# Issuing the attention part's weight loads from ScalarE's queue instead of SyncE's

## The chip, the cores and the metric

The kernel runs on one core of a Trainium2 chip. The time is device time of one execution in microseconds (us). Names used below: PE is TensorE (matrix products), DVE is VectorE, ACT is ScalarE, POOL is GpSimd and SP is SyncE, which here only issues DMAs.

## The reference

Three computations follow each other; the second and third take the output of the one before as `x`.

```python
# attention: q, k, v are (2, 8, 768, 64); blocks of 32 keys, window of 16
k_sum = k.reshape(B, H, nb, block, D).max(axis=3)
v_sum = v.reshape(B, H, nb, block, D).mean(axis=3)
scores_l = scale * np.matmul(q, k.transpose(0, 1, 3, 2))      # kept where |i - j| < window
scores_s = scale * np.einsum('bhsd,bhnd->bhsn', q, k_sum) + np.log(block)
a = softmax over [scores_l (masked), scores_s]
x = np.matmul(a, np.concatenate([v, v_sum], axis=2))          # -> (1536, 512)
# first feed-forward part: w_in 512 x 2048, w_out 2048 x 512
h = x @ w_in
x = (h - np.tanh(h)) @ w_out
# second: w1, w2 512 x 1024, w3 1024 x 1024, w_out 1024 x 512
out = ((x @ w1) * (x @ w2)) @ w3 @ w_out
```

Inputs and outputs are float32.

## The kernel before

All weights come to the chip as 64-bit words and are turned into float32 by the engines. A **unit** is one 128 x 512 block of a weight; there are 72, in a fixed order (first `w3` and the last `w_out`, whose product is formed during attention, then `w_in`, `w_out`, `w1`, `w2`). A unit goes through these steps, all in class `Weights`:

- `load`: a DMA of 512 KB into one of four buffers `raw` (`NRAW = 4`).
- `start`: ACT forms `bits` (in some units `dec`) from the words' upper halves (L112).
- `dve`: three DVE instructions (L115, L117, L119) make the float32 block `dec`. The third is the last that reads `raw`.
- `high`: ACT rounds it to `wh` (L147). `low`: POOL forms the rest `wl` (L154).

Attention runs in 28 steps `g` (0 to 27), a loop written out by hand; the order in which the code names instructions is each engine's order. A step works on several groups of four tiles at once: scores of group g + 1 (PE, `s`), softmax of group g (DVE `pr`, `nm` at L374, then four exponentials on ACT at L377), transposes of g - 2 (PE, `t`, L391) and their copy to SBUF at the end of the step (ACT, `pt`, L396), values of g - 3 (PE, `av`, L406), the split of the result of g - 4 (ACT `xh` at L417, DVE `xl`). There is one PSUM tile for `t`, so the transposes of a step wait until ACT has copied those of the step before. Three steps make one pair of heads. Beside this a step decodes one unit; steps 15, 18, 21, 24 and 25 start two (`MORE`). Pieces of the weight product (`w34a`) fill PE.

SP issues all DMAs, in the order of the code: keys `kt`, queries `qt`, values `vg`, the block means' rows (`vg` from `vr`, three small DMAs a pair), and the weights' `raw`. `load` lets a unit's DMA go when fewer than four buffers are taken:

```python
while len(self.raws) < min(n, len(self.units), self.n_dve + NRAW):
```

`n_dve` counts units whose three DVE instructions have been issued; `dve` calls `load` right behind the third. So the DMA that refills a buffer stands in SP's queue as soon as the code has named that third instruction, and SP waits there until DVE has executed it.

Of the kernel before, what the change touches and what calls it, by code (L numbers as in the profile page):

```python
# [46 lines left out]
NRAW = 4  # L47
# [10 lines left out]
def fused_kernel(tc, qT, kT, vW, w_in, w_out, w1, w2, w3, wo2, out):  # L58
    nc = tc.nc
    mm = nc.tensor.matmul  # L60

    class Weights:


        def __init__(self):
            self.units, self.index, self.raws, self.t, self.parts = [], {}, [], [], []
            self.free, self.place, self.ahead, self.psum, self.one = [], [], 1, None, False
            self.ops = []
            self.n_dve = self.n_high = self.n_low = 0

        def add(self, key, src):
# [17 lines left out]
            return place, *(pool.tile([P, 512], dt, tag=t, bufs=bufs, name=f"{name}_{i}") for i, t in enumerate((th, tl)))  # L89

        def load(self, n):
            while len(self.raws) < min(n, len(self.units), self.n_dve + NRAW):
                raw = rawp.tile([P, 512], U64, tag="raw", name=f"raw_{len(self.raws)}")
                nc.sync.dma_start(out=raw, in_=self.units[len(self.raws)])
                words = raw[:, :].bitcast(U32).rearrange("p (n two) -> p n two", two=2)
                self.raws.append((words[:, :, 0], words[:, :, 1]))

# [26 lines left out]
        def dve(self, k=1):  # L124

            for _ in range(k):
                if self.n_dve == len(self.t):
                    return False
                self.ops[self.n_dve].pop(0)()
                if not self.ops[self.n_dve]:  # L130
                    self.n_dve += 1
                    self.load(len(self.t) - 1 + self.ahead)
            return True

        def unit(self, k=1):
# [32 lines left out]
    wt = Weights()  # L168
# [30 lines left out]
    with tc.tile_pool(name="base", bufs=1) as base, \  # L199
# [79 lines left out]
        with tc.tile_pool(name="p1", bufs=1) as p1, \  # L279
# [4 lines left out]
            def load_k(n):  # L284
                kt[n] = p1.tile([P, SG], F32, tag="kt", bufs=3, name=f"kt_{n}")
                w = NQ // 2 * CW
                for i in ((0, w), (w, SG)) if n == 0 else ((0, SG),):
                    nc.sync.dma_start(out=kt[n][:, i[0]:i[1]], in_=kT[n // NP, n % NP, :, i[0]:i[1]])

            def load_q(n):  # L290
                qt[n] = p1.tile([P, S], F32, tag="qt", bufs=2, name=f"qt_{n}")
                w = TU * QT
                for i in ((0, w), (w, S)) if n == 0 else ((0, S),):
                    nc.sync.dma_start(out=qt[n][:, i[0]:i[1]], in_=qT[n // NP, n % NP, :, i[0]:i[1]])

            def load_vwin(n):
                vg[n] = p1.tile([P, NQ, P], F32, tag="vg", bufs=3, name=f"vg_{n}")
                nc.sync.dma_start(out=vg[n], in_=vW[n // NP, n % NP])
# [38 lines left out]
            def block_rows(n):  # L337
                w = NB // NBR
                for c in range(NBR):
                    nc.sync.dma_start(out=vg[n][QT + c * w:QT + (c + 1) * w, :, :],  # L340
                                      in_=vrow[n][c * BLK:c * BLK + w, :].unsqueeze(1).to_broadcast([w, NQ, P]))
# [8 lines left out]
            def scores(g):  # L350

                nonlocal n_s
                n, u = divmod(g, NU)
                st[g] = []
                for _ in range(1 + (g >= ALL)):
                    tag = "extra" if g >= ALL and n_s % 3 == 2 else "s"
                    n_s += g >= ALL
                    st[g].append(ps1.tile([P, TU, NC], F32, tag=tag, bufs=2 if tag == "s" else 1, name=f"s_{g}_{n_s}"))
                wt.one = g >= ALL
                for i in range(TU):  # L360
                    t = u * TU + i
                    for hf in range(2):
                        r = slice(hf * QT, (hf + 1) * QT)
                        mm(out=st[g][i % len(st[g])][half_of(g, i, hf), i, :], lhsT=qt[n][r, t * QT:(t + 1) * QT],
                           rhs=kt[n][r, t * CW:t * CW + NC], start=True, stop=True)
# [76 lines left out]
            for g in range(NG + 4):  # L442
                n, u = divmod(g, NU)
                parts = list(range(n34, min(n34 + N34[g], 32)))
                n34 += len(parts)

                if u == (0 if n else 2) and n + 2 < NN:
                    load_k(n + 2)
                if u == 1 and n + 1 < NN:
                    load_vwin(n + 1)  # L450
                if u == 2 and 0 < n < NN:
                    block_rows(n)
                if u == 2 and n + 2 < NN:
                    load_q(n + 2)

                late = g + 1 >= ALL
                if g + 1 < NG and not late:
                    scores(g + 1)
                for i in parts[:0 if late else 1]:
                    w34_part(i)  # L460
                if 0 <= g - 2 < NG:
                    transposes(g - 2)
                for i in parts[0 if late else 1:]:
                    w34_part(i)
                if g + 1 < NG and late:
                    scores(g + 1)
                if 0 <= g - 4 < NG:
                    x_high(g - 4)
                for i in list(pvs):
                    value_copy(i)  # L470
                if g == 1:
                    value_blocks(0, ps1.tile([P, TU * QT + P], F32, tag="av", bufs=1, name="pvs")[:, TU * QT:])
                if g == 2:
                    block_rows(0)
                if 0 <= g - 3 < NG:
                    rest = values(g - 3)
                    if u == 0 and n < NN:
                        value_blocks(n, rest)
                if g < 2:
                    busy(4)  # L480

                wt.high()
                wt.low()
                for i in range(TU):
                    if g < NG:
                        softmax_a(g, (0, 2, 1, 3)[i] if g >= ALL else i)
                    if i == 1 and 1 <= g <= NG:
                        softmax_b(g - 1)
                    if i == 2 and 0 <= g - 4 < NG:
                        x_low(g - 4)  # L490
                    if i and g < NG + 3:
                        wt.dve(1)
                if g - 1 in MORE:
                    wt.unit()
                if g == NG:
                    wt.psum = None
                if g < NG + 3:
                    wt.start(2 if g in MORE else 1)
                if n + 1 < NN:
                    for i in ((0, 1), (2,), ())[u] if n else ((), (0, 1, 2), ())[u]:  # L500
                        key_blocks(n + 1, i)
                if 0 <= g - 2 < NG:
                    probs(g - 2)
                wt.ahead = min(NRAW, g + 2)
                for i in parts:
                    w34_end(i)
# [405 lines left out]
```

## Time and profile before

| | |
|---|---|
| runs | 582.7, 582.71, 581.56 us, median 582.7 |
| profiled execution, span | 583.9 us |
| PE busy in the span | 567.7 us, 97% |
| DVE, ACT, POOL busy | 463.0, 339.4, 281.2 us |
| DMA | 56.56 MB, mean 97 GB/s |

The profile shows one execution; its span is the time from its first to its last instruction, and nothing of it lies outside. It is 1.2 us longer than the median of the runs. A busy share is a mean over stages that differ much, so the stages have to be read apart.

### The profile page before, as it was taken

Reading aid. Unit: us, or ns where it says so; the run is one execution under the profiler, and the core shown is the slowest. Engines: PE = TensorE matmul, PEld = TensorE weight load, DVE = VectorE, ACT = ScalarE, POOL = GpSimd, SP = SyncE. Lnnn points to the kernel's source line nnn. Section 1 sums busy time; section 2 is a strip of 40 time slices with the busy share of each in tenths; the row PEclk is TensorE's granted clock in tenths of the full one; section 3 lists DMA queues with packets and bytes.
Section 4 is the critical chain, followed back from the end, with each engine's and each line's share of the span. In section 5 each row is a group of like instructions: output and inputs, shape, how many; then the busy total and the mean of one; then the engine's idle time right before and its main releaser. Section 6 shows DMA issues by size and latency. Waiting matters only on the chain.

```text
span 583.9 us, 9222 instructions
## 1 busy us (share of the span) xinstructions
PE 567.7 (97%) x3240; PEld 459.6 (79%) x3240; DVE 463.0 (79%) x885; ACT 339.4 (58%) x741; POOL 281.2 (48%) x239
## 2 busy tenths in 40 slices
PE   7999899999999999999999999999999999999997
PEld 5777677777688888888888888888887887888885
DVE  4699998876999999779999978999658587778610
ACT  3599988856788786466767566764324322213110
POOL 4366555552555655324646522547725644616320
PEclk9999999999999999999999999999999999999999
DMA  8889977540333223012223101233000100000021
GB/s 317 278 299 290 305 243 212 150 158 22 107 107 108 82 100 109 0 36 74 88 93 90 56 1 39 86 92 109 0 1 1 60 13 1 1 1 0 1 90 54
DMA packets 18526, 56.56 MB, mean 97 GB/s; under 512 B 1968, under 2 KB 4656, under 8 KB 18480
## 3 DMA queue, kind: packets, MB, share of 16 engines
q1 hardware_dynamic: 18480, 55.98, 29.4%
q8 instruction: 25, 0.41, 0.3%
q14 instruction: 21, 0.17, 0.1%
HBM read 51.64 MB, written 3.15 MB: 94 GB/s over the span
## 4 chain that ended last, share of the span: by engine, by line
PE 73%; DVE 13%; issue 6%; ACT 4%; DMA 2%; POOL 1%; SPq 0%; DVEq 0%; POOLq 0%; ACTq 0%
PE x L191 6%; PE x L192 6%; PE x L190 6%; PE ph L190 6%; PE ph L192 6%; PE ph L191 6%; PE p_w L190 4%; PE p_w L192 4%; PE p_w L191 4%; PE o L190 3%; PE o L192 3%; PE o L191 3%; PE w L192 2%; PE w L191 2%; PE w L190 2%
## 5 line engine op out<-in xcount | busy, mean ns | idle before, releaser
L154 POOL TENSOR_TENSOR wl<-dec,wh 128x512 fp32r<-128x512 f32 x72 | 110.8, 1543 | 55.1 <-ACT wh L147 51.2
L195 POOL TENSOR_TENSOR gl<-g,gh 128x512 fp32r<-128x512 f32 x48 | 65.2, 1359 | 133.4 <-ACT gh L550 70.9
L191 PE MATMUL x<-gl,wh 128*128 128x512 f32 x192 | 75.1, 391 | 1.7 <-POOL gl L195 1.7
L190 PE MATMUL x<-gh,wh 128*128 128x512 f32 x192 | 75.0, 390 | 0.1
L190 PE MATMUL ph<-xh,wh 128*128 128x512 f32 x192 | 74.8, 390 | 0.0
L192 PE MATMUL x<-gh,wl 128*128 128x512 f32 x192 | 74.7, 389 | 0.0
L192 PE MATMUL ph<-xh,wl 128*128 128x512 f32 x192 | 74.7, 389 | 0.0
L191 PE MATMUL ph<-xl,wh 128*128 128x512 f32 x192 | 74.7, 389 | 0.0
L119 DVE SCALAR_TENSOR_TENSOR dec<-raw,dec 128x512 uint32<-128x512 uint32 x48 | 62.8, 1309 | 1.6
L563 ACT ACTIVATE u<-ph 128x512 f32<-128x512 f32 x48 | 28.8, 599 | 47.9 <-PE ph L192 47.9
L147 ACT CAST wh<-dec 128x512 fp32r<-128x512 f32 x72 | 44.6, 623 | 17.8 <-DVE dec L119 17.6
L571 DVE TENSOR_TENSOR g<-ph,u 128x512 f32<-128x512 f32 x48 | 32.7, 682 | 21.0 <-ACT th L564 20.9
L377 ACT ACTIVATE pr<-pr,nm 128x120 f32<-128x120 f32 x96 | 37.1, 391 | 12.2 <-DVE nm L374 11.9
L191 PEld LDWEIGHTS x<-gl,wh 128*128 128x128 f32 x192 | 36.0, 188 | 10.2 <-POOL gl L195 2.7
L195 POOL TENSOR_TENSOR s_w<-s_w,s_w 128x512 fp32r<-128x512 f32 x16 | 22.9, 1450 | 43.5 <-ACT s_w L742 23.5
L555 DVE COPY_PREDICATED g<-mk,th 128x512 f32<-128x512 uint32 x48 | 39.7, 827 | 4.2 <-DVE g L573 0.5
L190 PEld LDWEIGHTS x<-gh,wh 128*128 128x128 f32 x192 | 36.0, 188 | 8.5 <-DVE x2a L599 0.5
L190 PEld LDWEIGHTS ph<-xh,wh 128*128 128x128 f32 x192 | 36.0, 188 | 7.6
L191 PEld LDWEIGHTS ph<-xl,wh 128*128 128x128 f32 x192 | 36.0, 188 | 7.5
L192 PEld LDWEIGHTS ph<-xh,wl 128*128 128x128 f32 x192 | 36.0, 188 | 7.4
L192 PEld LDWEIGHTS x<-gh,wl 128*128 128x128 f32 x192 | 36.0, 188 | 7.3
L573 DVE SCALAR_TENSOR_TENSOR g<-sq,g 128x512 f32<-128x512 f32 x48 | 39.3, 820 | 0.7 <-ACT sq L569 0.6
(157 smaller groups left out, 1422.2 us busy)
## 6 DMA issues: line engine op xcount, KB each, us to landing
raw<-w SPq DMA_DIRECT2D x32, 512.0 KB
raw<-w_in SPq DMA_DIRECT2D x16, 512.0 KB
raw<-w_out SPq DMA_DIRECT2D x16, 512.0 KB
vg<-vW SPq DMA_DIRECT2D x8, 768.0 KB
raw<-wo SPq DMA_DIRECT2D x8, 512.0 KB
kt<-kT SPq DMA_DIRECT2D x7, 544.0 KB
qt<-qT SPq DMA_DIRECT2D x7, 384.0 KB
out<-u_out SPq DMA_DIRECT2D x6, 256.0 KB
```

The costliest lines, as they stand in the source:

```text
L119: lambda tu=tu, su=su, lo=lo: stt(out=tu, in0=lo, scalar=29, in1=su, op0=ALU.logical_shift_right, op1=ALU.bitwise_or)])
L147: nc.scalar.copy(out=h, in_=self.t[n])
L154: nc.gpsimd.tensor_tensor(out=l, in0=self.t[self.n_low], in1=h[:, :].bitcast(F32), op=ALU.subtract)
L190: mm(out=acc, lhsT=lh, rhs=rh, start=start, stop=False)
L191: mm(out=acc, lhsT=lh, rhs=rl, start=False, stop=False)
L192: mm(out=acc, lhsT=ll, rhs=rh, start=False, stop=stop)
L195: eng.tensor_tensor(out=out, in0=x, in1=high.bitcast(F32), op=ALU.subtract)
L377: nc.scalar.activation(out=pr[g][:, i, :], in_=pr[g][:, i, :], func=AF.Exp, scale=-1.0, bias=nm[g][:, i:i + 1], accum_out=z[g][:, i:i + 1])
L555: nc.vector.copy_predicated(out=g, mask=mask[:, :].bitcast(U32), data=t)
L563: nc.scalar.activation(out=u, in_=ph, func=AF.Square)
L571: nc.vector.tensor_tensor(out=gn, in0=ph, in1=u, op=ALU.mult)
L573: nc.vector.scalar_tensor_tensor(out=gn, in0=sq, scalar=GAM, in1=gn, op0=ALU.add, op1=ALU.mult)
```

## The change

The DMAs of the units from the third on, as long as attention lasts (up to step 23), are issued by ACT. `load` is no longer called when DVE's third instruction has been named, but once a step, behind `low`, and by `start`. In the attention part the limit is no longer `n_dve` but `safe`, the value that `n_dve` had behind `low` of the step. Keys, queries, values and block rows stay on SP, and so do the first two units and all from step 24 on.

```diff
-            self.ops = []
+            self.ops, self.safe = [], 0
...
         def load(self, n):
-            while len(self.raws) < min(n, len(self.units), self.n_dve + NRAW):
+            early = self.psum is not None
+            while len(self.raws) < min(n, len(self.units), (self.safe if early else self.n_dve) + NRAW):
                 raw = rawp.tile([P, 512], U64, tag="raw", name=f"raw_{len(self.raws)}")
-                nc.sync.dma_start(out=raw, in_=self.units[len(self.raws)])
+                (nc.scalar if early and len(self.raws) > 1 else nc.sync).dma_start(out=raw, in_=self.units[len(self.raws)])
...
                 if not self.ops[self.n_dve]:
                     self.n_dve += 1
-                    self.load(len(self.t) - 1 + self.ahead)
+                    if self.psum is None:
+                        self.load(len(self.t) - 1 + self.ahead)
...
                 wt.high()
                 wt.low()
+                wt.load(len(wt.t) - 1 + wt.ahead)
+                wt.safe = wt.n_dve
```

What it does to the order, at three places. Lines of the changed kernel are numbered one to four higher than those of the kernel before. The numbers behind the names count tiles, so the same unit may have another number before and after. In brackets stand the semaphores that a row waits for: `DVE`, `PE`, `Activation`, `Pool` are counted by an engine, `DMAHW` and a digit by earlier DMAs.

ACT in step 6 before: a rounding, the four exponentials, `bits` of the unit loaded three steps ago, the copy `pt`.

```order
L147 CAST wh_568<-dec_457 128x512 [waits DVE_49]
L377 ACTIVATE pr_573,z_574<-pr_573,nm_572 128x120 [waits DVE_49] x4
L112 ACTIVATE bits_593<-raw_387 128x512 [waits DMAHW4_49]
L396 COPY pt_598<-t_541 120x512 [waits PE_49,Activation_49]
L417 CAST xh_124<-av_547 128x256 [waits PE_49]
```

ACT in step 6 with the change:

```order
L149 CAST wh_566<-dec_455 128x512 [waits DVE_49]
L379 ACTIVATE pr_571,z_572<-pr_571,nm_570 128x120 [waits DVE_49] x4
L95 DMA raw_588<-wo 128x512 [waits DMAHW5_49,Activation_49]
L113 ACTIVATE bits_591<-raw_453 128x512 [waits DMAHW6_49]
L398 COPY pt_596<-t_539 120x512 [waits PE_49,Activation_49]
L419 CAST xh_124<-av_545 128x256 [waits PE_49]
```

One DMA stands between the last exponential and `bits`. There are 27 such DMAs on ACT in all: one or two in steps 1 to 23.

ACT in steps 23 and 24 before. `raw_1757` and `raw_1762` are the two units that step 24 starts; SP issued them in steps 21 and 22.

```order
L377 ACTIVATE pr_1812,z_1813<-pr_1812,nm_1811 128x120 [waits DVE_49] x4
L112 ACTIVATE bits_1832<-raw_1687 128x512 [waits DMAHW1_49,DVE_49]
L396 COPY pt_1834<-t_1774 120x512 [waits PE_49,Activation_49]
L417 CAST xh_126<-av_1794 128x256 [waits PE_49]
L147 CAST wh_1863<-dec_1764 128x512
L112 ACTIVATE dec_1876<-raw_1757 128x512 [waits DMAHW2_49,Pool_49]
L112 ACTIVATE dec_1878<-raw_1762 128x512 [waits DMAHW3_49,Pool_49]
L396 COPY pt_1880<-t_1836 120x512 [waits PE_49]
```

ACT in steps 23 and 24 with the change:

```order
L379 ACTIVATE pr_1808,z_1809<-pr_1808,nm_1807 128x120 [waits DVE_49] x4
L95 DMA raw_1825<-w_out 128x512 [waits DMAHW5_49,Activation_49]
L95 DMA raw_1827<-w_in 128x512 [waits Activation_49]
L113 ACTIVATE bits_1830<-raw_1758 128x512 [waits DMAHW2_49,DVE_49]
L398 COPY pt_1832<-t_1770 120x512 [waits PE_49,Activation_49]
L419 CAST xh_126<-av_1790 128x256 [waits PE_49]
L149 CAST wh_1861<-dec_1760 128x512
L113 ACTIVATE dec_1876<-raw_1825 128x512 [waits DMAHW5_49,Pool_49]
L113 ACTIVATE dec_1878<-raw_1827 128x512 [waits DMAHW6_49,Pool_49]
L398 COPY pt_1880<-t_1834 120x512 [waits PE_49]
```

The two units of step 24 are issued in step 23, as a pair. Steps 17 and 20 issue a pair in the same way, for steps 18 and 21.

SP around steps 14 to 17 before: each group of keys, values or block rows stands behind a weight load that waits for DVE.

```order
L340 DMA vg_801<-vr_1025 8x12x128 [waits DMAHW4_49]
L294 DMA qt_1072<-qT 128x768 [waits DMAHW5_49,PE_49]
L94 DMA raw_1127<-w 128x512 [waits DMAHW6_49,DVE_49,Activation_49]
L288 DMA kt_1136<-kT 128x1088 [waits DMAHW7_49,Pool_49]
L94 DMA raw_1211<-w 128x512 [waits DMAHW0_49,DVE_49,Activation_49]
L298 DMA vg_1223<-vW 128x1536 [waits DMAHW1_49,PE_49]
L94 DMA raw_1286<-w 128x512 [waits DMAHW2_49,DVE_49,Activation_49]
L94 DMA raw_1291<-w 128x512 [waits DMAHW3_49,DVE_49,Activation_49]
L340 DMA vg_1002<-vr_1253 8x12x128 [waits DMAHW4_49,PE_49,Activation_49]
```

SP at the same place with the change:

```order
L342 DMA vg_799<-vr_1023 8x12x128 [waits DMAHW3_49]
L296 DMA qt_1070<-qT 128x768 [waits DMAHW5_49,PE_49]
L290 DMA kt_1134<-kT 128x1088 [waits DMAHW6_49,Pool_49]
L300 DMA vg_1221<-vW 128x1536 [waits DMAHW7_49,DMAHW1_49,PE_49]
L342 DMA vg_1000<-vr_1251 8x12x128 [waits DMAHW1_49,PE_49,Activation_49]
```

The weight loads with their waits for DVE are gone from SP here; the rest keeps its order.

## Rows read from the trace of the kernel before

**Rows 1.** Stretch, us, busy PE, PEld, DVE, ACT, POOL (count), PE clock, DMA share, GB/s.

```profile
23.50:74.00 50.50, 46.32 (x594) 36.65 (x595) 47.47 (x199) 46.77 (x161) 30.20 (x30) 1.00 0.92 304
74.00:131.00 57.00, 54.60 (x579) 42.73 (x579) 48.28 (x147) 43.63 (x129) 31.88 (x28) 1.00 0.62 187
131.00:583.90 452.90, 447.34 (x1956) 365.97 (x1954) 357.71 (x499) 240.30 (x423) 210.27 (x143) 1.00 0.16 53
```

**Rows 2.** Waits of ACT, 23.5 to 74: us in total, times, longest.

```profile
ACT pr L377 <- DVE nm L374: 2.5, 8, 0.5
```

**Rows 3.** Waits of all engines, 5 to 131: us in total, times, longest.

```profile
PE t L391 <- ACT pt L396: 3.3, 5, 0.9
...
PE av L406 <- DMA vg<-vr: 1.0, 1, 1.0
...
ACT bits L112 <- DMA raw<-w: 0.6, 1, 0.6
```

**Rows 4.** Waits of SP's DMA queue, 23.5 to 131.

```profile
SPq L94 <- DVE dec L119: 85.3, 28, 15.0
```

**Rows 5.** Line 94: DMA issues, ns min/median/max, first and last start.

```profile
L94 SPq DMA_DIRECT2D raw<-w x32: 327/328/1634, 4.6 to 404.6; - x32
```

**Rows 6.** Timeline of SP's issues at four places: start us, us, instruction.

```profile
34.49 0.33 SPq L94 DMA_DIRECT2D raw<-wo  x1
34.92 0.38 SPq L288 DMA_DIRECT2D kt<-kT  x1
...
109.48 0.33 SPq L94 DMA_DIRECT2D raw<-w_out  x1
111.93 0.33 SPq L94 DMA_DIRECT2D raw<-w_in  x1
...
150.74 0.33 SPq L94 DMA_DIRECT2D raw<-w_out  x1
```

**Rows 7.** Timeline of ACT in step 6; in brackets idle time ahead and its cause.

```profile
37.69 0.40 ACT L377 ACTIVATE pr<-pr,nm 128x120 f32<-128x120 f32 x1 [0.18 <-DVE nm L374]
...
38.08 0.64 ACT L112 ACTIVATE bits<-raw 128x512 f32<-128x512 f32 x1
```

**Rows 8.** Line 396 from 36.5 to 39 us: ns, start; ACTq is ACT's sequencer.

```profile
L396 ACTq EVENT_SEMAPHORE  x1: 17/17/17, 37.7 to 37.7; - x1
L396 ACT COPY pt<-t x1: 575/575/575, 38.7 to 38.7; 120x512 f32<-120x512 f32 x1
```

**Rows 9.** Timeline of ACT and PE around the end of step 17.

```profile
84.12 0.40 ACT L377 ACTIVATE pr<-pr,nm 128x120 f32<-128x120 f32 x1 [0.65 <-DVE nm L374]
...
84.71 0.66 ACT L112 ACTIVATE bits<-raw 128x512 f32<-128x512 f32 x1
...
86.03 0.62 PE L391 MATMUL t<-ident,pr 128*120 128x128 f32 x4 [0.73 <-ACT pt L396]
```

**Rows 10.** Line 112 from 83 to 85 us.

```profile
L112 ACTq EVENT_SEMAPHORE  x1: 17/17/17, 84.1 to 84.1; - x1
```

**Rows 11.** Half microseconds behind the lone load at 150.74, columns as in rows 1.

```profile
151.00:151.50 0.50, 0.50 (x4) 0.42 (x3) 0.50 (x2) 0.50 (x2) 0.10 (x1) 1.00 0.00 0
...
153.50:154.00 0.50, 0.42 (x1) 0.11 (x1) 0.50 (x2) 0.50 (x2) 0.49 (x1) 1.00 0.09 33
```

**Rows 12.** Timeline of ACT and PE, steps 23 to 25.

```profile
114.51 0.40 ACT L377 ACTIVATE pr<-pr,nm 128x120 f32<-128x120 f32 x1 [0.42 <-DVE nm L374]
...
116.94 1.24 ACT L112 ACTIVATE dec<-raw 128x512 f32<-128x512 f32 x2
118.09 0.56 ACT L396 COPY pt<-t 120x512 f32<-120x512 f32 x1
...
120.32 0.65 PE L391 MATMUL t<-ident,pr 128*120 128x128 f32 x4
```

**Rows 13.** The stretch with the highest DMA rate, columns as in rows 1.

```profile
10.00:15.00 5.00, 4.83 (x26) 3.42 (x24) 4.31 (x17) 3.80 (x16) 0.99 (x1) 1.00 1.02 420
```

**Rows 14.** Groups of DVE's instructions, 23.5 to 74: busy us, mean ns, idle ahead.

```profile
L117 DVE SCALAR_TENSOR_TENSOR bits<-raw,bits 128x512 uint32<-128x512 uint32 x13 | 8.9, 686 | 0.0
```

## The prediction, made before the changed kernel ran

> **What bounds the kernel now.** I read the stretches first [rows 1]. Behind 131 us TensorE (PE) is busy 447.34 of 452.90 us, nothing moves to ScalarE there, and only a later start of that part could change it. From 74 to 131 us PE is busy 54.60 of 57.00. From 23.5 to 74 us no engine is full: PE 46.32, VectorE (DVE) 47.47 and ScalarE (ACT) 46.77 of 50.50, and DMA has its highest share, 0.92. There DVE sets the pace and ACT follows closely: ACT's idle time is mostly the wait of the step's fourth exponential for its maximum, 2.5 us in 8 waits [rows 2].
>
> Then the waits from 5 us to 131 us [rows 3]. The reader is to see how few name a DMA: PE once for the rows of block means, 1.0 us, and ACT once for a weight load, 0.6 us. Keys and queries are in neither row. SyncE's queue does spend 85.3 us waiting for DVE's last decode step before it may refill a weight buffer [rows 4], and keys, queries and values stand behind these waits; but nothing behind them was late except the one row of 1.0 us. What PE does wait for is ACT's copy of the transposed probabilities: 3.3 us in 5 waits. Three of these lie in steps 17, 20 and 23.
>
> **What the change removes.** SyncE's queue loses 27 of its loads and their waits, so keys, values and block rows are issued earlier. Worth at most the 1.0 us of PE above. PE and ACT then had slack: that wait lies in the stretch that DVE paces. I take 0. The Trainium skill says in "DMA: Bandwidth & Descriptors", section "Issuing engines are not separate DMA queues", that DMAs of several engines run on the same 16 DMA engines and that issuing from more of them saves only the sequencer's issue time. By that rule the gain is 0 too, and the waits in the trace agree: SyncE's time was not what anyone waited for.
>
> **What it adds on ACT.** 27 issues. ACT issued no DMA before, so the price is bounded by SyncE's: a weight load's issue takes 328 ns in the median, 1634 ns at most [rows 5], and two in a row start 0.43 us apart [rows 6]. I take 0.33 and 0.43, since no wait for space in a queue is likely with one or two loads of 512 KB in ACT's own.
>
> Do they lie beside ACT's work? In step 6 the fourth exponential starts at 37.69, its accumulator is read, and `bits` starts at 38.08 [rows 7]. So 0.39 us pass in which the engine works and its sequencer is free. That the sequencer does run ahead can be seen from an instruction that only the sequencer executes: the semaphore wait ahead of the copy `pt` stands at 37.7, while the copy runs at 38.7 [rows 8]. It was held up to the exponential's release (37.69), then passed it, the accumulator read and `bits` at once. In step 17 the same: the exponential is released at 84.12, and the wait ahead of `bits` stands at 84.1 [rows 9, 10]. So an issue that stands between the exponential and `bits` begins about at the exponential's release and ends 0.33 us later, under the 0.39 us that the engine needs. One issue costs 0 in all steps with one. If this cover were gone, each would push `bits`, `pt`, `xh` and `wh` back by 0.43 us; behind them wait DVE's `xl`, GpSimd's low part and PE's transposes.
>
> Steps 17, 20 and 23 issue two. Both end at 0.05 + 0.43 + 0.33 = 0.81 us behind the release. In step 17 `bits` starts now 0.59 us behind it (84.71), so it moves by 0.22 us, `pt` too, and PE's transposes, which start at 86.03 after waiting 0.73 us for `pt` [rows 9], start that much later. PE goes on from there without slack. 3 x 0.22 = 0.66 us.
>
> The issues carry waits of their own: for a DMA some eight places earlier in the program, which by the steps landed long before, and for ACT's own reading of the buffer. They no longer wait for DVE, since a load is issued only when DVE was done a step before. I take 0.
>
> **What it moves: loads come later.** A buffer is refilled a step later than before, two steps ahead of its use where one unit is started a step. A step lasts 50.5 / 13 = 3.9 us in the first stretch [rows 14]. What a lone load takes: issued at 150.74, its bytes flow from 151.5 to about 153.6 [rows 6, 11], 2.9 us. In time, also with keys and values beside it. But where steps start two units, the lead is one step. The tight one is step 24: its two loads were issued at 109.48 and 111.93 [rows 6]; now both leave ACT in step 23, behind the exponential released at 114.51, that is at 114.55 and 115.0. They are wanted at 116.94 and, 0.57 us on, 117.51 [rows 12]. The first lands at 114.55 + 2.9 = 117.45 at the earliest. The second follows in the same queue, with a third load on SyncE's queue beside it: at best 512 KB more at 420 GB/s [rows 13], 1.25 us, so 118.7; if all three (1.57 MB, 3.75 us at that rate, flowing from 115.4) share, 119.2, and 0.4 us for its slow beginning gives 119.6. So `pt`, at 118.09 now, starts between 119.3 and 120.2 and ends 0.56 us later, at 119.9 to 120.8. PE's transposes of step 25 start at 120.32 now; with step 23's 0.22 they would at 120.54. More delay: 0 to 0.35 us, I take 0.15.
>
> **The sum.** 0 - 0 + 0.66 + 0.15 = +0.8 us. The profiled execution has 583.9 us; it becomes 584.7. It lies 1.2 us above the median of the runs, 582.7, so for runs 583.5 us.
>
> **The rivals.** *ACT pays each issue in full (slower).* If `bits` can't be prepared during an issue and the engine stands still, the double issues cost 84.12 + 0.39 + 2 x 0.43 - 84.71 = 0.66 us each [rows 9], 2.0 us together. The 13 single ones in the first stretch (13 decodes, so 13 steps [rows 14]) cost 13 x 0.43 = 5.6 us, less ACT's idle time there, 50.50 - 46.77 = 3.7 [rows 1]: 1.9. Busy records overlap a little (the exponential's ends at 37.69 + 0.40 = 38.09, `bits` starts at 38.08, with the reading of the accumulator between them [rows 7]), so there is more idle time than that; I take 1.0. With 0.4 of step 24: +3.4 us, 586.1. It decides from an issue time of about 0.45 us on. Against it stand rows 8 and 10; for it, that no DMA was ever seen on this engine.
>
> *The sequencer isn't even held by the exponential.* Then both issues of a pair are over before it is released and steps 17, 20 and 23 lose nothing; step 24's loads leave some 0.5 us earlier, and nothing is left: 582.7. The Trainium skill draws it so in "Perfetto Trace Analysis", section "Per-instruction lifecycle: what the profiler-reported window actually captures": ScalarE instructions are pushed into a wait queue, and the sequencer decodes on while they wait. The trace disagrees in part: 84.1 in rows 10 is the release, not earlier.
>
> *Loads are late at more places.* Values are now issued when PE frees their buffer, in step 17 beside two weight loads. 768 KB more in front of the second one is 1.8 us at 420 GB/s; if PE had no slack there, and step 24 took its worst, +1.5 to +2 us, 584.5.
>
> *Unblocked keys and values pay (faster).* The 1.0 us of PE's wait goes, and ACT's wait behind it: -1.0 us, 581.7; to be faster beyond what can be told it would need a second such place, and no row shows one.
>
> **How the numbers follow.** Within 0.2% (1.2 us, about what a measurement of this kernel tells from no change) are 581.5 to 583.9. Chances: the forecast 0.42, of which 0.08 ends above; the sequencer fully ahead 0.13; ACT pays in full 0.28, all above; late loads 0.07, above by a half; faster 0.10, of which 0.07 by more than 0.2%. Sums: faster 0.07, same 0.53, slower 0.40. The forecast's own range is 582.7 to 584.3. The 8 in 10 must reach to the rival at 586.1 and nearly to the one at 581.7, so 581.8 to 586.2.
>
> **What would show it.** On ACT: DMA issues of 0.33 us in the profile that lie beside the exponential, `bits` 0.39 us behind the fourth exponential's start in steps 3 to 13 as now (0.8 says the rival is right). In steps 17, 20, 23: PE's wait for `pt` longer by about 0.2, in step 17 from 0.73 [rows 9]. In step 24: ACT waits for two weight loads, 0.5 to 2 us, and PE's transposes of step 25 start with a small wait. The start of the feed-forward part shifts by what the end shifts. Wrong would make it: an issue on ACT much longer than on SyncE, or a wait for a landing inside ACT's queue, which stops the exponentials behind it.

## The result, and the profile after

| | before | changed | ratio, 95% interval |
|---|---|---|---|
| first measurement, median us | 582.13 | 588.74 | 1.0109 [1.0082, 1.0136] |
| second, another chip (`after_2`) | 583.02 | 588.76 | 1.0103 [1.0077, 1.0128] |

The change costs 5.7 to 6.6 us. The forecast was 583.5, its range ended at 586.2. The first profile of the changed kernel has a span of 589.2 us; it is the longest of its four executions (the others: 586.6 to 586.7). So `after_2`, span 586.6, is shown where the two differ.

The stretches of the changed kernel; columns as in [rows 1].

```profile
23.50:74.00 50.50, 45.08 (x569) 36.03 (x570) 43.23 (x183) 42.84 (x147) 27.45 (x28) 0.92 0.86 284
74.00:131.00 57.00, 50.17 (x546) 38.83 (x545) 46.17 (x145) 41.15 (x127) 28.54 (x27) 1.00 0.54 174
131.00:589.20 458.20, 452.73 (x1992) 370.33 (x1990) 361.35 (x503) 243.45 (x429) 214.18 (x145) 1.00 0.17 54
```

Behind 131 us PE is as full as it was in [rows 1]; the loss lies ahead of it. PE, DVE and ACT are all less busy in both earlier stretches, so they wait. For what, the waits from 5 to 131 us say:

```profile
PE t L393 <- ACT pt L398: 10.7, 9, 2.1
...
ACT dec L113 <- DMA raw<-w: 3.0, 1, 3.0
PE av L408 <- DMA vg<-vr: 2.8, 1, 2.8
...
ACT bits L113 <- DMA raw<-wo: 2.1, 1, 2.1
...
ACT bits L113 <- DMA raw<-w: 1.7, 2, 1.1
...
ACT dec L113 <- DMA raw<-w_in: 1.4, 1, 1.4
...
ACT dec L113 <- DMA raw<-w_out: 0.7, 1, 0.7
```

Against [rows 3]: ACT now waits 8.9 us for weight words, where it waited 0.6; PE waits 10.7 us for `pt` instead of 3.3, and 2.8 instead of 1.0 for the block rows.

A single issue is what the prediction took it for. ACT's timeline in step 7:

```profile
43.09 0.40 ACT L379 ACTIVATE pr<-pr,nm 128x120 f32<-128x120 f32 x1 [0.43 <-DVE nm L376]
43.16 0.34 ACTq L95 DMA_DIRECT2D raw<-wo  x1
...
43.54 0.63 ACT L113 ACTIVATE bits<-raw 128x512 f32<-128x512 f32 x1
```

It starts 0.07 us behind the exponential's release, lies beside it, and `bits` follows 0.45 us behind that release instead of 0.39 [rows 7].

To place the loss I use one landmark of every kernel: the start of the copy `pt` in step 15, and the start of ACT's first work on the feed-forward part (`u`). What lies between them I call the late stretch, what lies ahead of the first the start. What follows the second takes 452.8 to 453.0 us in all 18 profiles, so nothing is lost there.

```
                       pt step 15   first u   late stretch
before (rows' profile)    74.81     130.87       56.06
changed, first profile    75.61     136.34       60.73
changed, after_2          75.37     133.60       58.23
```

In the first profile 2.5 us of the late stretch belong to that execution alone: above all, in step 17 one DMA issue took 1.23 us, and step 18 waited 2.96 us for a load. ACT's timeline there:

```profile
85.43 1.23 ACTq L95 DMA_DIRECT2D raw<-w  x1
...
93.68 0.66 ACT L113 ACTIVATE dec<-raw 128x512 f32<-128x512 f32 x1 [2.96 <-DMA raw<-w]
```

`after_2` has neither (but other kernels have such long issues, see `tiny`). So the late stretch costs 2.2 us (58.23 - 56.06), and the start the other 3.6 of the 5.7 us by which the medians on that chip differ.

The profile of before hid that. Its own execution is a long one: in the runs of the kernel before that list both, the time is 1.7 to 1.8 us above the span, so a span of 583.9 belongs to a time of about 585.6, some 3 us above the median. Its late stretch and what follows are as long as in `late_on_sp`, the fastest kernel below, so those 3 us lie in its start. (The forecast's 1.2 us between span and median compare two measures; it did no harm, since what counts is the 0.8 us that it added to the median.)

### The profile page after: what moved, and what is told of

It is laid out like the page before. It is cut to its first block, busy times and chain, and to the rows that moved or that the text cites. A ratio compares the mean times of both kernels' runs of the same rounds, so it can differ in the third digit from the quotient of the medians.

```text
span 589.2 us, 9209 instructions
## 1 busy us (share of the span) xinstructions
PE 564.1 (96%) x3240; PEld 457.1 (78%) x3240; DVE 463.9 (79%) x885; ACT 339.3 (58%) x741; POOL 280.9 (48%) x239
## 4 chain that ended last, share of the span: by engine, by line
PE 66%; DVE 6%; issue 4%; ACT 3%; DMA 1%; POOL 1%; ACTq 0%; DVEq 0%; POOLq 0%
PE x L193 6%; PE x L192 6%; PE x L194 6%; PE ph L192 6%; PE ph L193 6%; PE ph L194 6%; PE p_w L192 4%; PE p_w L194 4%; PE p_w L193 4%; PE o L194 4%; PE o L192 4%; PE o L193 4%; PE w L194 2%; PE w L192 2%; PE w L193 2%
## 5 line engine op out<-in xcount | busy, mean ns | idle before, releaser
L575 DVE TENSOR_TENSOR g<-ph,u 128x512 f32<-128x512 f32 x48 | 32.7, 682 | 21.2 <-ACT th L568 21.1
L197 POOL TENSOR_TENSOR s_w<-s_w,s_w 128x512 fp32r<-128x512 f32 x16 | 22.8, 1446 | 43.5 <-ACT s_w L746 23.5
```

The source lines that it names most:

```text
L197: eng.tensor_tensor(out=out, in0=x, in1=high.bitcast(F32), op=ALU.subtract)
L575: nc.vector.tensor_tensor(out=gn, in0=ph, in1=u, op=ALU.mult)
```

## Experiments

All times are medians in us; each ratio is to the kernel before, measured between the same rounds on the same chip. The medians of the kernel before on these four chips are 582.88 to 583.02.

| kernel | loads issued by ACT | time | ratio, 95% interval | late stretch |
|---|---|---|---|---|
| `late_on_sp` | none, changed rule | 580.89 | 0.9972 [0.9958, 0.9986] | 56.07 |
| `late_on_sp_2` | the same, another chip | 581.14 | 0.9969 [0.9951, 0.9988] | 56.10 |
| `tiny` | none; 26 of 2 KB besides | 588.0 | 1.0087 [1.0051, 1.0124] | 59.10 |
| `first_on_sp` | from unit 5 | 586.5 | 1.0058 [1.0040, 1.0075] | 58.24 |
| `five` | from unit 3, five buffers | 586.77 | 1.0067 [1.0046, 1.0088] | 57.11 |
| `five_first` | from unit 5, five buffers | 585.55 | 1.0035 [1.0017, 1.0054] | 57.17 |
| `act_early` | units 3 to 12 | 585.18 | 1.0028 [0.9999, 1.0057] | 56.07 |
| `act_late` | from unit 13 | 584.86 | 1.0038 [1.0011, 1.0066] | 58.15 |
| `three_on_sp` | none, three buffers | 583.13 | 1.0005 [0.9980, 1.0031] | 55.49 |
| `filled` | from unit 3 | 586.89 | 1.0061 [1.0038, 1.0085] | 58.20 |
| `swap` | from unit 3, issued earlier | 585.52 | 1.0034 [1.0014, 1.0055] | 56.04 |
| `swap_first` | from unit 5, issued earlier | 583.84 | 1.0012 [0.9992, 1.0033] | 56.06 |
| `swap_six` | from unit 7, issued earlier | 583.18 | 1.0011 [0.9992, 1.0029] | 56.06 |
| `swap_twelve` | from unit 13, issued earlier | 582.05 | 0.9983 [0.9969, 0.9998] | 56.08 |

**Queue or rule.** `late_on_sp` keeps the rule and gives the loads back to SyncE:

```diff
-                (nc.scalar if early and len(self.raws) > 1 else nc.sync).dma_start(out=raw, in_=self.units[len(self.raws)])
+                nc.sync.dma_start(out=raw, in_=self.units[len(self.raws)])
```

> The changed rule (once a step, limit `safe`) with every load on SyncE again. Theory (a load on ScalarE can leave only when ScalarE's own program comes to it, while SyncE runs ahead of the program and lets it go when its buffer is free): the loads leave as early as in the kernel before, and the time is 582 to 583 us. Rival (the rule itself makes the loads late): 586 to 589 us, with ScalarE waiting for loads as in the changed kernel.

580.89: the theory holds, and the kernel is even faster than before. So the whole loss comes with ACT's queue, and the rule alone is a gain. Where it comes from is seen around the second group of block rows. First a second profile of the kernel before (`before_again`, 585.54 us, span 583.8).

> The kernel before, unchanged, for a second profile. The shown one has a slow start: TensorE's products at about half their later pace until 21 us. If that differs from execution to execution, this one starts faster and its span is about 3 us shorter, 580 to 582 us; if it belongs to the kernel, 583.5 us or more.

Its timeline of ACT, where the rows are copied:

```profile
25.37 0.26 ACT L335 COPY vr<-av 96x128 f32<-96x128 f32 x1
```

The timeline of SyncE behind it:

```profile
27.59 0.33 SPq L94 DMA_DIRECT2D raw<-w  x1
28.02 2.19 SPq L340 DMA_DIRECT2D vg<-vr  x3
```

And of PE, where they are used:

```profile
36.71 1.12 PE L406 MATMUL av<-pt,vg 120*64 120x64 f32 x16 [2.44 <-DVE nm L374]
```

The rows are ready at 25.63, but a weight load stands ahead of them on SyncE and leaves at 27.59, when VectorE has freed its buffer; the rows leave at 28.02. PE then waits 2.44 us at 36.71 for its values. The wait is put down to a maximum that had long been there; so it was for something else, and the rows are the likeliest. (Up to here this execution is ahead of the first profile of before; the stall takes that back, and the spans come out alike. So the slow first 20 us do differ from execution to execution, as the theory has it, but its span of 580 to 582 us was missed: here the 3 us are lost in another way.) With the rule on SyncE (`late_on_sp_2`) the load is named behind the rows. ACT's timeline there:

```profile
25.80 0.26 ACT L337 COPY vr<-av 96x128 f32<-96x128 f32 x1
```

SyncE's:

```profile
26.09 2.19 SPq L342 DMA_DIRECT2D vg<-vr  x3
```

PE's:

```profile
35.12 0.69 PE L408 MATMUL av<-pt,vg 120*64 120x64 f32 x16 [0.42 <-DMA vg<-vr]
```

The rows leave 0.03 us behind the copy, and PE waits 0.42 us. In both executions PE starts some 9 us behind the rows' leaving (8.7 and 9.0), which supports that it was the rows. But `before_again` is one execution, and the cause of the 0.3% is so far argued from it; in the profile of before the second to fourth group leave 2.9 to 3.2 us behind their copies, and PE waits only once, 1.0 us.

**The price of issues.** `tiny` is the kernel before, and ACT issues small DMAs whose data nobody reads:

```diff
+                    if i == 3 and 1 <= g < 24:
+                        for _ in range(1 + (g in (17, 20, 23))):
+                            tiny = p1.tile([P, 4], F32, tag="tiny", bufs=4, name=f"tiny_{g}_{_}")
+                            nc.scalar.dma_start(out=tiny, in_=qT[0, 0, :, :4])
```

> The kernel before, all loads on SyncE, with one more DMA of 2 KB issued by ScalarE behind the fourth exponential of steps 1 to 23 (two in steps 17, 20 and 23): the price of the issues alone. Forecast's step (an issue lies beside the exponential): 582 to 583 us. Rival (ScalarE pays each issue in full): 585 to 586 us.

588.0, beyond both. A lone issue lies beside an exponential, as in step 7 above. The second issue of the three pairs doesn't. ACT's timeline:

```profile
33.30 0.40 ACT L377 ACTIVATE pr<-pr,nm 128x120 f32<-128x120 f32 x1 [0.18 <-DVE nm L374]
33.30 0.34 ACTq L490 DMA_DIRECT2D tiny<-qT  x1
...
83.97 1.48 ACTq L490 DMA_DIRECT2D tiny<-qT  x1
...
100.71 0.90 ACTq L490 DMA_DIRECT2D tiny<-qT  x1
...
116.59 0.93 ACTq L490 DMA_DIRECT2D tiny<-qT  x1
```

The late stretch is 3.0 us longer than before, and all of it falls on the double issues: ACT's `bits` behind them waits 1.47, 0.94 and 1.03 us, and from the copy `pt` of step 16 to that of 19, from 19 to 22 and from 22 to 23 it takes 1.3, 0.8 and 0.9 us more than before. That leaves some 2 us of the 5.1, in the start. The waits of SyncE's queue from 5 to 131 us (total, times, longest):

```profile
SPq L294 <- DMA vg<-vW: 6.6, 3, 3.3
...
SPq L294 <- DMA tiny<-qT: 4.6, 1, 4.6
```

And its timeline:

```profile
26.32 2.91 SPq L340 DMA_DIRECT2D vg<-vr  x3
33.90 0.33 SPq L294 DMA_DIRECT2D qt<-qT  x1
```

SyncE stood still from 29.23 to 33.90, until a 2 KB transfer that nobody needs, issued by ACT at 33.30, had landed. The program's DMAs share a few counters (the `DMAHW` in the order), and by the order a DMA waits for the one that used its counter before. Two queues are coupled in this way: in this run SyncE could not run ahead of ACT's place in the program. What this costs isn't shown; PE has no wait for queries in this profile. So the run shows a coupling of its own, and behind step 15 it prices a double issue at about 1 us where the second one is long. In the changed kernel SyncE's waits for other DMAs come to 2 to 3 us in the two profiles, and no queries wait for a DMA.

**Lateness alone.** `three_on_sp` skips every fourth raw buffer, with all loads on SyncE:

```diff
-            while len(self.raws) < min(n, len(self.units), (self.safe if early else self.n_dve) + NRAW):
+            while len(self.raws) < min(n, len(self.units), (self.safe - 1 if early else self.n_dve) + NRAW):
                 raw = rawp.tile([P, 512], U64, tag="raw", name=f"raw_{len(self.raws)}")
+                if early and len(self.raws) % 3 == 2:
+                    rawp.tile([P, 512], U64, tag="raw", name=f"gap_{len(self.raws)}")
```

> Every load on SyncE, but three buffers for raw words during attention instead of four, so that each load leaves about a step later than in the version with all loads on SyncE, and ScalarE issues nothing. Theory (lateness alone costs, whoever issues): ScalarE waits for raw words in the steps behind 15, and the time is 585 to 589 us. Rival (ScalarE's queue is the cause): 580.5 to 582.5 us.

583.13, about 2 us above the same kernel with four buffers (0.3% by the ratios), and nothing lost in the late stretch. The forecast time was missed, but the run hardly tests the theory there: the two loads of step 24 leave 5.3 and 3.8 us ahead of the copy `pt` of step 23, before 6.2 and 3.8, in `after_2` 1.5 and 1.1. A buffer fewer on SyncE, which lets a load go when the buffer is free, is not what the change did.

**Start and late stretch apart.** Two halves of the change, by the number of the unit (`1 < len(self.raws) < 12`, and `len(self.raws) > 11`):

> The changed kernel with only units 3 to 12 issued by ScalarE, the later ones by SyncE. Theory (two separate losses: about 5.5 us by step 4, from the loads of units 3 and 4 and the block rows, and 4.7 us behind step 15, from loads that ScalarE's place in the program makes late): 584 to 587 us, no wait of ScalarE for raw words in steps 16, 18 and 24. Rival (the loss grows with the number of issues on ScalarE): with 10 of 27 issues 583 to 584 us.

> The other half: units 3 to 12 issued by SyncE, the later ones by ScalarE. Theory: the start as in the kernel with all loads on SyncE (580.9 us), then waits for raw words in steps 16, 18 and 24 as in the changed kernel, 4 to 5 us: 584 to 586 us. Rival (all of the loss is in the start): 580.5 to 582 us. Rival (it grows with the issues, 17 of 27): 585 to 586 us, with waits spread over the steps.

585.18 and 584.86. Against 580.89 with none that is 4.3 and 4.0 us, together 8.3; the whole change has 7.6 to 7.9 (by the ratios 7.1 and about 8). So there are two losses that about add up. In `act_early` the late stretch is whole (56.07), in `act_late` it has the 2.1 us of the changed kernel. The other 1.8 us of `act_late` are not explained; they are about as large as the uncertainty of the two ratios. In its profile 1.5 us are lost in step 5, where PE waits 2.0 us for GpSimd's part of the keys (1.3 in `late_on_sp`) and the granted clock falls to 0.50, some 20 us before ACT's first load.

**The late stretch.** `five` adds a fifth raw buffer while attention lasts:

```diff
-            while len(self.raws) < min(n, len(self.units), (self.safe if early else self.n_dve) + NRAW):
+            while len(self.raws) < min(n, len(self.units), (self.safe if early else self.n_dve) + NRAW + (len(self.raws) < 34)):
...
+                k = len(self.raws)
+                extra = k < 30 and k % 5 == 4
+                raw = (p1 if extra else rawp).tile([P, 512], U64, tag="raw5" if extra else "raw",
+                                                   bufs=1 if extra else NRAW, name=f"raw_{k}")
...
-                wt.ahead = min(NRAW, g + 2)
+                wt.ahead = min(NRAW + 1, g + 2)
```

> The changed kernel with a fifth buffer for raw words during attention, so that ScalarE issues each load a step earlier from step 4 on. Theory (late loads in steps 16, 18 and 24 are the loss, 4 us of it): ScalarE's waits for raw words behind 74 us fall from 7.7 us to below 1, and the time is 584 to 585.5 us. Rival (the issues themselves and their place in ScalarE's queue are the loss): 587.5 to 589 us.

ACT waits 0.2 us for weight words, not 8.9 (behind 74 us that was 6.2, not the 7.7 of the theory), and of the 2.2 us 1.05 stay: steps 17, 20 and 23 are longer by 0.34, 0.29 and 0.39 us. That is the price of three double issues whose second one is short. The total, 586.77, was expected lower; the missing part lies in the start. `after_2` shows both parts. ACT's timeline in step 17:

```profile
84.71 0.39 ACT L379 ACTIVATE pr<-pr,nm 128x120 f32<-128x120 f32 x1 [0.65 <-DVE nm L376]
84.78 0.33 ACTq L95 DMA_DIRECT2D raw<-w  x1
...
85.20 0.39 ACTq L95 DMA_DIRECT2D raw<-w  x1
85.70 0.63 ACT L113 ACTIVATE bits<-raw 128x512 f32<-128x512 f32 x1 [0.49 <-DVE dec L120]
```

ACT's in step 24:

```profile
119.30 0.68 ACT L113 ACTIVATE dec<-raw 128x512 f32<-128x512 f32 x1 [0.63 <-DMA raw<-w_out]
121.78 0.66 ACT L113 ACTIVATE dec<-raw 128x512 f32<-128x512 f32 x1 [1.80 <-DMA raw<-w_in]
122.34 0.57 ACT L398 COPY pt<-t 120x512 f32<-120x512 f32 x1
```

PE's behind it:

```profile
123.06 0.62 PE L393 MATMUL t<-ident,pr 128*120 128x128 f32 x4 [1.02 <-ACT pt L398]
```

The second issue ends at 85.59, 0.88 us behind the release; `bits` starts 0.11 later. Together 0.99 instead of 0.59 [rows 9]: 0.40 us. In step 24 both loads are late, 2.43 us together (no wait in [rows 12]); PE waits 1.02 us, and the way from `pt` of step 23 to `u` is 1.1 us longer (16.30 us, 15.19 before).

`swap` exchanges the two new lines, so that from step 4 on the loads stand ahead of the exponentials:

```diff
-                wt.load(len(wt.t) - 1 + wt.ahead)
                 wt.safe = wt.n_dve
+                wt.load(len(wt.t) - 1 + wt.ahead)
```

> The changed kernel with the two new lines exchanged, so that from step 4 on ScalarE issues each load ahead of the four exponentials of a step instead of behind them, some 1.6 us earlier, beside the rounding copy. The number of issues stays. Theory (double issues behind the fourth exponential cost 0.3 us each and the landings of step 24 come too late, 2.1 us together behind step 15): the stretch from the transposes' copy of step 15 to the first ScalarE work on the feed-forward part shrinks from 58.2 us (the half with the later loads on ScalarE) to 56.1 to 56.8, and the time is 584 to 586 us, the loss of the start being left. Rival (issues cost wherever they stand): 58 us there, time 587 to 589 us.

The late stretch is 56.04, as before, with one issue more (28): in step 17 the pair now lies beside the rounding copies, and nobody behind step 15 waits for a landing. So the place of the issues, and the earlier landings that go with it, were the late loss. The time, 585.52, keeps the loss of the start. ACT's timeline of `swap` in step 17:

```profile
80.99 0.62 ACT L149 CAST wh<-dec 128x512 fp32r<-128x512 f32 x1
81.15 0.33 ACTq L95 DMA_DIRECT2D raw<-w  x1
...
81.58 0.39 ACTq L95 DMA_DIRECT2D raw<-w  x1
```

**The start.** ACT's timeline in the changed kernel, first profile:

```profile
13.18 0.38 ACTq L95 DMA_DIRECT2D raw<-wo  x1
...
14.61 0.33 ACTq L95 DMA_DIRECT2D raw<-wo  x1
...
17.30 0.34 ACTq L95 DMA_DIRECT2D raw<-w  x1
...
19.90 0.62 ACT L113 ACTIVATE bits<-raw 128x512 f32<-128x512 f32 x1 [2.12 <-DMA raw<-wo]
```

SyncE's, with the first block rows:

```profile
15.08 2.54 SPq L342 DMA_DIRECT2D vg<-vr  x3
```

PE's, with the values that need them:

```profile
25.09 1.12 PE L408 MATMUL av<-pt,vg 120*64 120x64 f32 x16 [2.83 <-DMA vg<-vr]
```

And stretches of 2 us, columns as in [rows 1], PE's clock third from the end:

```profile
18.00:20.00 2.00, 1.13 (x18) 0.81 (x16) 0.75 (x6) 0.10 (x1) 0.00 (x0) 1.00 1.11 390
...
26.00:28.00 2.00, 2.00 (x29) 1.37 (x27) 0.00 (x0) 0.00 (x0) 0.00 (x0) 0.50 0.64 260
```

The third unit's load has no one to wait for; SyncE let it go at 6 to 7 us, ACT only when its program came to it, at 13.18, and then waited for it. The first block rows leave SyncE at 15.08, among the loads of 14.61 and 17.30, and PE gets its values at 25.09, 10.0 us later. With everything on SyncE (`late_on_sp`) the rows leave at 15.16 and PE starts at 20.78, 5.6 us later. SyncE's timeline:

```profile
15.16 2.34 SPq L342 DMA_DIRECT2D vg<-vr  x3
17.54 1.30 SPq L95 DMA_DIRECT2D raw<-wo  x1
```

PE's:

```profile
20.78 0.69 PE L408 MATMUL av<-pt,vg 120*64 120x64 f32 x16 [0.81 <-DMA vg<-vr]
```

The loss falls in one step. The copy `pt` of step 3 starts at 23.48 in `after_2` and at 22.98 in `late_on_sp`, which waits 0.95 us for its fourth unit; that of step 4 at 32.67 and 26.46, that of step 15 at 75.37 and 70.08. So ACT's wait of 2.1 us for the third unit has cost little by step 3; what costs is the wait for the rows and what follows it.

In PE's stalls (2.05 us until 21.2, 2.83 us until 25.1) the granted clock falls to 0.50, the 1.2 GHz level; it is 1.00 again from 32 us on. `filled` puts idle products into the stall:

```diff
+                if g == 3:
+                    busy(4)
                 if 0 <= g - 2 < NG:
                     transposes(g - 2)
+                if g == 3:
+                    busy(4)
```

> The changed kernel with 4 more idle products of TensorE ahead of the transposes and 4 ahead of the values of step 3, 4.3 us at full pace, in front of the two waits of 2.05 and 2.83 us behind which the granted clock falls to 0.5. Theory (the fall of the clock costs about 2 us in the start): the clock stays at 1.00 there, time 585 to 587 us. Rival (the fall costs nothing, since DMA sets the pace there): 588.5 us or more.

One of the stretches of `filled` there:

```profile
24.00:26.00 2.00, 2.00 (x52) 1.73 (x50) 1.25 (x9) 0.62 (x4) 0.00 (x0) 1.00 1.02 411
```

In the profiled execution the clock stays at 1.00 there, and the median is 586.89, 1.9 us below the changed kernel's; the two intervals just overlap. The eleven executions show it better: seven have a mean clock of 0.999 or more and spans of 583.1 to 585.4 (middle 584.2), four have 0.994 to 0.996 and 585.3 to 587.1 (middle 586.5). All ten of the changed kernel have 0.997 or less. The step itself can be read too: from PE's start on the values to the copy `pt` of step 4 it takes 7.8 us in `after_2` (24.85 to 32.67) and 5.1 in `filled` (23.80 to 28.89), and `after_2` wins back 0.5 by step 6. So the fall of the clock is some 2 us of the start's loss.

`first_on_sp` leaves units 3 and 4 with SyncE (`len(self.raws) > 3`), `five_first` does it with five buffers, `swap_first` with the exchanged lines:

> The changed kernel with units three and four issued by SyncE as well. Theory (the late third unit holds ScalarE 2.1 us, and the rows of block means, which share the DMA engines with later loads, hold TensorE 2.8 us, whose clock then falls): both waits shrink below 0.5 us and the time is 585.5 to 587.5 us. Rival (what is lost there is won back by step 15, the loss lies in the steps behind): 588.2 to 589 us.

> The changed kernel with a fifth buffer for raw words and units 3 and 4 on SyncE. Theory: ScalarE waits for no weight load, three double issues remain, 1.0 us behind step 15; time 582 to 584.5 us. Rival (a second queue beside the block rows): 584.5 to 586 us.

> The same with units 3 and 4 on SyncE. Theory (the two late early units hold ScalarE and TensorE in steps 2 and 3; without them the start is that of the kernel before, in its slower executions): 581.5 to 584 us. Rival (weight loads on a second queue beside the rows of block means hold TensorE in steps 3 to 6 whichever unit it is): 584 to 586 us, with the clock below 0.998 in all runs.

586.5, 585.55 and 583.84: 1.7 to 2.3 us less each for `first_on_sp` against the changed kernel and for `swap_first` against `swap`; `five_first` missed its theory by an us, and its 585.55 lies in the rival's range. `first_on_sp` met the range but not the mechanism: PE still waits 1.5 us for the first rows, and ACT 3.1 us for a load, now in step 3. The same wait stands in `swap_first`, on ACT:

```profile
17.34 0.38 ACTq L95 DMA_DIRECT2D raw<-w  x1
...
17.93 0.87 ACTq L95 DMA_DIRECT2D raw<-wo  x1
24.31 0.62 ACT L113 ACTIVATE bits<-raw 128x512 f32<-128x512 f32 x1 [3.34 <-DMA raw<-wo]
```

SyncE's timeline:

```profile
16.84 0.93 SPq L95 DMA_DIRECT2D raw<-wo  x1
```

ACT's in `late_on_sp`:

```profile
22.41 0.64 ACT L113 ACTIVATE bits<-raw 128x512 f32<-128x512 f32 x1 [0.95 <-DMA raw<-wo]
```

SyncE issued the load that is waited for at 16.84, ahead of both; ACT has it 7.5 us later. In `late_on_sp`, where no load is on ACT's queue, it left at 17.54 and ACT used it at 22.41, 4.9 us later. The fourth unit takes 3.6 to 5.1 us in the eight profiles in which ACT waits for it and has issued no weight load beside it, and 5.8, 7.2 and 7.5 in the three in which it has (`five_first`, `first_on_sp`, `swap_first`). So loads for later steps have shared with it. The Trainium skill says in "DMA: Bandwidth & Descriptors", section "Queues, rings and completion order", that each DMA engine goes round robin between the queues that have work. The trace agrees, 7.5 against 4.9 us.

The rest of the series takes ACT's first load later, `len(self.raws) > 5` and `> 11`, with the exchanged lines:

> Exchanged lines (each load ahead of the exponentials), and units 3 to 6 on SyncE: ScalarE's first load leaves in step 4 instead of step 2. Theory (SyncE's one queue moves things in the order in which they are needed; loads that ScalarE adds at 17 us share with the earlier ones and make a unit that is wanted at 21 us land at 24): ScalarE's wait for raw words in step 3 falls from 3.3 us to below 1.5, time 1 to 2 us below that of the version with units 3 and 4 on SyncE, 581.5 to 583 us. Rival (any load on ScalarE costs the same, 24 or 22 of them): 583.5 to 584.5 us.

> Exchanged lines, and units 3 to 12 on SyncE; 15 or so loads stay on ScalarE. Theory (start as with all loads on SyncE, nothing lost behind step 15): the same as all loads on SyncE on this chip within 1 us, 580.5 to 582 us, and 56.1 us from the copy of step 15 to the feed-forward part. Rival (the issues themselves cost): 582.5 to 584 us.

> All loads on SyncE with the changed rule, once more, as the other end of the series on one chip (units on SyncE: 2, 6, 12, all). Theory (block rows no longer stand behind a load that waits for VectorE, and leave 2 us earlier): 1.0 to 2.0 us below the kernel before, 580.5 to 581.5 us. Rival (the 0.28 per cent of the first measurement belong to its chip): within 0.5 us of before.

> The changed kernel itself on the same chip, for a second profile and as the first end of the series. Theory (2.1 us behind step 15 in every execution, the rest in the start, and 2.5 us in step 18 in the profiled execution alone): 587.5 to 589 us, 58.1 us behind step 15. Rival (step 18's wait belongs to the kernel): 60.7 us there.

Units on SyncE at the start 2, 4, 6, 12, all: ratios 1.0034, 1.0012, 1.0011, 0.9983, 0.9969 (the first two from another chip). In `swap_six` ACT's wait of 3.34 us in step 3 is gone (0.3 is left), as the theory has it, but the median, 583.18, is above the theory's range; from 4 units to 6 nothing is gained that can be told. `swap_twelve`, 582.05, ends at the edge of its theory's range, 1.0 us below before, with 18 loads on ACT. `late_on_sp` has the lowest median, on two chips, and issues none there; its interval overlaps that of `swap_twelve`.

## Why the prediction was wrong

- **A lone issue costs nothing**: right. It is 334 ns in the median, lies beside the exponential (43.16 behind 43.09), and no price shows: from the copy `pt` of step 6 to that of step 15, with a lone issue in each step, `after_2` takes 35.60 us, `late_on_sp_2` with none 35.68. The price in full, +3.4 us, is excluded for it.
- **Double issues, 0.66 us**: right in mechanism, too small: 1.05 us. The second issue ends 0.88 us behind the release, not 0.81, and `bits` needs another 0.11, which was left out. That the second can be much longer, as in `tiny`, wasn't foreseen.
- **Step 24, 0.15 us**: too small, 1.1 us. `pt` came 5.04 us behind that of step 23, 2.63 more than before (2.41), not 1.2 to 2.1.
- **"In time, also with keys and values beside it"**: this is the step that failed. Loads were asked for lateness only where steps start two units; the start, steps 1 to 4, was not looked at. There SyncE had let the third unit's load go at 6.84 us (profile of before), ACT only at 13.18. That, the sharing of two queues and the fall of the clock in the stall cost 3.6 us net, and 5.5 against `late_on_sp_2` on the same chip (7.6 less 2.1 of the late stretch). The rival "loads are late at more places" had the mechanism, but looked for it in step 17 and priced it at 584.5.
- **Unblocked SyncE, worth 0**: wrong, and the second failure: 1.9 to 2.0 us by `late_on_sp` and `late_on_sp_2` (0.28 and 0.31%). The likeliest cause is the block rows: the 1.0 us wait in [rows 3] is one of a later group, in `before_again` the wait is 2.44 us and the clock falls behind it. That this gives the whole 1.9 us isn't shown. "PE and ACT then had slack" was read from one execution.
- **The issues' own waits, 0**: right for the changed kernel, where ACT waits for no key, value or row; `five` has one, 1.6 us for block rows ahead of a `bits`, which reads none.
- **The sequencer held until the release**: right, 43.16 behind 43.09 and 84.78 behind 84.71, not earlier.
- **The range** ended at 586.2 because of ACT paying in full, which did not occur in the changed kernel; no case in it had the start.

What stays open: which transfers in steps 4 to 10 make `swap_six` slower than `swap_twelve`; how much of the sharing in the start comes from the third unit's late issue, since its bytes then flow beside the rows; and why the second issue of a pair is sometimes long.

## What to carry to other kernels

SyncE, which only issues DMAs here, let a load go 6 to 7 us before ScalarE came to the same place in the program (6.02 to 6.84 against 13.18). So before loads are moved, look at how far ahead of their place they leave now, in the start above all, where queues are empty of waits. Loads on a second queue shared the bandwidth with those on the first: what was ordered by need in one queue was no longer ordered, and loads for later delayed one for now (7.5 us instead of 4.9). If the issues do stand on a computing engine, put them beside long instructions, ahead of the work that others wait for (`swap`), and find out first whether another order on the old queue does as much: here it gave 0.3% where the move cost 1%.

## What the runs showed of the hardware

- The same kernel starts at two paces. In the profile of before PE's group `s` takes 1.87 us at 20.52, in `before_again` 1.04 us at 20.21, both with a granted clock of 1.00. Products at half pace with the clock granted in full were not expected, and the runs don't settle why.
- A PE stall of some 3 us in the start went with about 7 (`after_2`) and 10 us (first profile) at a granted clock of 0.50 in the changed kernel, and with means of 0.60 and 0.55 for 4 us in `before_again`; with idle products in the stall there was no fall in the profiled execution of `filled`.
- A DMA of 2 KB on ACT held SyncE for 4.6 us, through a shared counter.
- The second issue of a pair on ACT takes 0.39 to 0.45 us in `after_2`, `five` and `swap`, but 0.90 to 1.48 in `tiny`, 1.23 in the first profile of the changed kernel, 1.30 and 0.93 in `swap_six` and `swap_first` (step 20), and 0.50 to 0.69 in step 17 of `act_late`, `filled` and `first_on_sp`; a lone one takes 334 ns in the median. The runs don't settle why.
